# An attention and one-expert kernel: the gates of all tokens computed as if no row were routed, parked in DRAM, two rows replaced there, and reloaded

## The chip, the cores and the metric

The kernel runs on one core of one Trainium2 chip. The metric is the device time of one execution in microseconds (us); the median of three runs of the kernel before is 795.93 us (792.62 to 797.04). Profile times count from the start of the profiled span.

## What is computed

Token rows `x` (2048 rows of 640 values) are normalized to `xn`. Two branches work on `xn`, and the output joins them:

```python
xn = _layernorm(x)
s  = attention(xn)                    # 32 heads of 192, the last 512 keys of a cache, then @ wo
# the routed branch
r   = xn @ w_r                        # one score a token
idx = argsort(-r)[:2]                 # the two best tokens
y   = (silu(x_sel @ w_gate) * (x_sel @ w_up)) @ w_down * sigmoid(r_sel)
z   = xn with y added to the rows idx # 2046 rows stay xn
out = x + s * silu(z)
```

So the gate `silu(z)` is a function of `xn` alone in all rows but two. The kernel uses `silu(z) = z/2 * (1 + tanh(z/2))`.

## The kernel before, in words

**Steps and blocks.** The attention is done in 64 steps: 8 groups of 4 heads, 4 stretches of 512 tokens, 2 pairs of heads. Each step has two halves, called blocks here, numbered 0 to 127. Block b computes scores, exps and products for 256 tokens (two row tiles, a = 0 and 1) and two heads. Blocks 0 to 11 and the last two have an order of their own, written out by hand; blocks 12 to 125 run in the order of the list `BLOCK` (L927). Nothing is reordered: each engine executes its instructions as the program issues them.

```python
BLOCK = "A S0 M0 W m E0 B S1 M1 P E1 l".split()
```

- `A`, `B`: the two phases of the query products for the next step (`q_phase`, L340); after `B`, ScalarE copies them out (L352). Their PSUM pool has one buffer, so the next `A` waits for that copy. Even blocks make two thirds of the query tiles (copy of 1024 columns), odd blocks one third.
- `S0`, `S1`: scores (L367) into one of two PSUM buffers. `M0`, `M1`: row maxima on VectorE (L372). `E0`, `E1`: exps on ScalarE (L377), into one of two buffers `pexp`; behind `E1` SyncE issues the DMA transpose `pT` (L383). The exps of block b+2 write the buffer that the `pT` of block b reads, so they wait for its landing.
- `P`: products with the values for block b-2 (L406), their scaling on VectorE (L413, L417) and ScalarE (L420), and the DMA transpose `oT` (L423).
- `W`: 24 products with `wo` for block b-6 (L447), and their addition to `s_acc` on VectorE (L470). The start of these 24 is used below as the start of a block, W(b).
- `m`, `l` and the middle of `P` are hooks for other work. The lists `mid[b]` run at `m`, after `W` and before `E0` and `M1`; `bg[b]` inside `P` (L948), between its two halves; `end[b]` and then `loads[b]` at `l`.

In `loads` SyncE issues the next group's keys, values and weights (192 to 288 KB each) and `kT` transposes. All these DMAs and both transposes stand in one SyncE queue, in program order.

**The routed branch** (lines 649 to 900) is laid into the hooks. `m_r` makes one column of `r` (L672). `m_round` (L681, mid[28]) rounds it to bf16; `m_rows` (bg[28]) turns it to 16 rows of 128 on TensorE through the query pool (L690) and copies it out on VectorE (L692). `m_top` (end[29]) takes the best of each row (L698 to L703) and spreads them by two GpSimd DMAs; `m_sel`, `m_tok`, `m_own` (end[31], mid[32], end[33]) find the two tokens, and an indirect GpSimd DMA gathers their rows of `x` (L741). `m_gather` (mid and end of 34 to 40) makes a mask `oh` of the two tokens (L758) and normalizes the two rows; its last piece, at mid[40], ends with L774 on VectorE, and loads[40] turns the rows (L778). `m_ffn` does three blocks of 512 hidden columns (bg[42], bg[49], bg[57]): products (L787), a copy and a tanh (L790, L791), one block later two VectorE operations (L797, L798) and a transpose `hT` on SyncE (L801). The weights come through ScalarE's queue. `m_down` (bg[62], bg[69]) and `m_sum` (bg[70]) make the two rows of `y`, put them into DRAM and load them back on all 128 partitions as `y_bc` (L846).

**The gates.** For each of the 16 row tiles n, `m_add(n)` at bg[71+2n] runs five GpSimd operations on `xn` (L850; L853 and L854 twice): halve it, and add each `y` times the mask. `m_gate(n)` then takes the tanh on ScalarE at bg[75+2n] (L860) and, at mid[76+2n], one VectorE operation that leaves the gate in `xn` (L863).

**The end.** From block 107 on, one tile a block: SyncE loads `x_fin` in loads[107+n] (L912), GpSimd makes `s_acc = s_acc * gate + x` at bg[109+n] (L917, L918). The last group's `W`, from block 118, multiplies its products by the gate (L473) and stores.

Of the kernel before, what the change touches and what calls it, by code (L numbers as in the profile page):

```python
# [8 lines left out]
ACT = mybir.ActivationFunctionType  # L9
# [12 lines left out]
def kernel(ctx, tc, A_x, A_k_cache, A_v_cache, A_wq, A_wo, B_x, B_w_r, B_w_gate, B_w_up, B_w_down, out):  # L22
# [149 lines left out]
    eps_t = const.tile([P, 1], FP32, name="eps_t")  # L172
    nc.vector.memset(eps_t, EPS)
    nc.vector.tensor_copy(out=ident, in_=ident_f)
    nc.gpsimd.memset(v_ring[:, :, :, Dh:Dh + 1], 1.0)

    mv = const.tile([P, NTB, 2], FP32, name="mv")
    rstd = const.tile([P, NTB], FP32, name="rstd")
# [470 lines left out]
    def m_open():  # L649
        late.close()  # L650
        M["stack"] = ExitStack()
        M["w"] = M["stack"].enter_context(tc.tile_pool(name="moe_w", bufs=1))
        M["s"] = M["stack"].enter_context(tc.tile_pool(name="moe_s", bufs=1))
        M["wr"] = M["s"].tile([P, D], BF16, name="wr_bc", tag="t3")
        nc.gpsimd.dma_start(out=M["wr"], in_=B_w_r.partition_broadcast(P))
        M["r"] = M["s"].tile([P, NTB], FP32, name="r_pn")
        M["xsT"] = M["s"].tile([P, DC, 32], BF16, name="xsT")
        M["xsel"] = M["s"].tile([32, D], BF16, name="xsel")
        nc.gpsimd.memset(M["xsel"], 0.0)
        M["pick"] = M["s"].tile([P, 2], FP32, name="pick")  # L660
        nc.gpsimd.memset(M["pick"], 0.0)
        for c in range(4):
            nc.gpsimd.affine_select(out=M["pick"], in_=M["pick"], compare_op=ALU.not_equal, fill=1.0, base=-32 * c,
                                    pattern=[[-1, 2]], channel_multiplier=1)
        M["oh"] = M["s"].tile([P, NTB, 2], FP32, name="oh")
        M["iota"] = M["s"].tile([P, NTB], FP32, name="iota")
        nc.gpsimd.iota(M["iota"], pattern=[[P, NTB]], base=0, channel_multiplier=1, allow_small_or_imprecise_dtypes=True)

    def m_r(n):
        def f():  # L670
# [6 lines left out]

    def m_round():

        M["r_b"] = M["s"].tile([P, NTB], BF16, name="r_b")  # L680
        nc.vector.tensor_copy(out=M["r_b"], in_=M["r"])  # L681
        M["base"] = M["s"].tile([NTB, 1], FP32, name="base")
        nc.gpsimd.iota(M["base"], pattern=[[0, 1]], base=0, channel_multiplier=P, allow_small_or_imprecise_dtypes=True)
        M["cpos"] = M["s"].tile([P, NCD], FP32, name="cpos")
        nc.gpsimd.iota(M["cpos"], pattern=[[1, NCD]], base=0, channel_multiplier=0, allow_small_or_imprecise_dtypes=True)

    def m_rows():

        r_ps = f_tile([NTB, P], BF16, "r_ps")
        nc.tensor.transpose(out=r_ps, in_=M["r_b"], identity=ident)  # L690
        M["rows"] = M["s"].tile([NTB, P], FP32, name="r_rows", tag="t2")
        nc.vector.tensor_copy(out=M["rows"], in_=r_ps)  # L692

    def m_top():

        top = M["s"].tile([NTB, 8], FP32, name="top8")
        loc = M["s"].tile([NTB, 8], U32, name="loc8")
        nc.vector.max(out=top, in_=M["rows"])  # L698
        nc.vector.max_index(out=loc, in_max=top, in_values=M["rows"])
        cand = M["s"].tile([NTB, 2, 2], FP32, name="cand")  # L700
        nc.vector.tensor_copy(out=cand[:, 0, :], in_=top[:, 0:2])
        nc.vector.tensor_copy(out=cand[:, 1, :], in_=loc[:, 0:2])
        nc.vector.tensor_scalar(out=cand[:, 1, :], in0=cand[:, 1, :], scalar1=M["base"][:, 0:1], scalar2=None, op0=ALU.add)  # L703
        c_d = tc.dram_tile([NTB, 2, 2], FP32, name="c_d")
        nc.gpsimd.dma_start(out=c_d, in_=cand)
        M["cand"] = M["w"].tile([P, NTB, 2, 2], FP32, name="cand_bc", tag="w")
        nc.gpsimd.dma_start(out=M["cand"].rearrange("p n k c -> p (n k c)"), in_=c_d.rearrange("n k c -> (n k c)").partition_broadcast(P))
# [24 lines left out]
    def m_own():  # L732
        sel = M["s"].tile([2, 2, 2], FP32, name="sel")
        for q in range(2):
            nc.vector.tensor_tensor(out=sel[:, q, :], in0=M["best"][0:2, q, :], in1=ident_f[0:2, 0:2], op=ALU.mult)
        M["own"] = M["s"].tile([2, 2], FP32, name="own")
        nc.vector.reduce_sum(out=M["own"], in_=sel, axis=AX.X)
        idx_i = M["s"].tile([2, 1], I32, name="idx_i")
        nc.vector.tensor_copy(out=idx_i, in_=M["own"][:, 1:2])
        M["xg"] = M["s"].tile([2, D], BF16, name="xg", tag="t2")  # L740
        nc.gpsimd.indirect_dma_start(out=M["xg"], out_offset=None, in_=x_f,  # L741
                                     in_offset=bass.IndirectOffsetOnAxis(ap=idx_i[:, 0:1], axis=0),
                                     bounds_check=S - 1)
# [9 lines left out]

    def m_gather():

        def mask():
            for j in range(2):
                nc.vector.tensor_scalar(out=M["oh"][:, :, j], in0=M["iota"], scalar1=M["best"][:, 1, j:j + 1], scalar2=0.5,  # L758
                                        op0=ALU.is_equal, op1=ALU.mult)

        def begin():
            M["mv2"] = M["s"].tile([2, 2], FP32, name="mv2")
            M["rs2"] = M["s"].tile([2, 2], FP32, name="rs2")
            ln_stats(M["xg"], M["mv2"], parts=2)
            M["nw"] = rsqrt_newton(M["mv2"][:, 1:2], M["rs2"][:, 0:1], 2, 1)

        def newton(q):
            for f in M["nw"][3 * q:3 * q + 3]:
                f()

        def apply():
            mv2, rs2 = M["mv2"], M["rs2"]
            ln_nmr(mv2[:, 0:1], rs2[:, 0:1], rs2[:, 1:2])
            nc.vector.tensor_scalar(out=M["xsel"][0:2, :], in0=M["xg"], scalar1=rs2[:, 0:1], scalar2=rs2[:, 1:2], op0=ALU.mult, op1=ALU.add)  # L774
        return [mask, begin] + [lambda q=q: newton(q) for q in range(4)] + [apply]

    def m_xsT():
        nc.sync.dma_start_transpose(out=M["xsT"], in_=M["xsel"])  # L778
# [2 lines left out]
    def m_ffn(fb):  # L781
# [12 lines left out]
        def act():  # L794
            th = M["th"]
            M["h"] = M["s"].tile([P, P], BF16, name="h")
            nc.vector.scalar_tensor_tensor(out=th[:, 2], in0=th[:, 2], scalar=1.0, in1=th[:, 0], op0=ALU.add, op1=ALU.mult)  # L797
            nc.vector.scalar_tensor_tensor(out=M["h"], in0=th[:, 2], scalar=0.5, in1=th[:, 1], op0=ALU.mult, op1=ALU.mult)  # L798

        def turn():  # L800
            nc.sync.dma_start_transpose(out=M["hT"][:, fb * 4:(fb + 1) * 4, :].rearrange("p c t -> p (c t)"), in_=M["h"])  # L801
# [10 lines left out]
    def m_sig():  # L812

        sg = M["s"].tile([P, 2], FP32, name="sg")
        nc.scalar.activation(out=sg, in_=M["best"][:, 0, :], func=ACT.Tanh, scale=0.5)
        nc.vector.tensor_scalar(out=sg, in0=sg, scalar1=0.5, scalar2=0.5, op0=ALU.mult, op1=ALU.add)
        nc.vector.tensor_tensor(out=M["pick"], in0=M["pick"], in1=sg, op=ALU.mult)
        M["wrow"] = M["s"].tile([P, 1], FP32, name="wrow")
        nc.vector.tensor_reduce(out=M["wrow"], in_=M["pick"], axis=AX.X, op=ALU.add)
# [15 lines left out]
    def m_sum():  # L835
# [4 lines left out]
        y_sb = M["s"].tile([2, D], BF16, name="y_sb", tag="t3")  # L840
        nc.gpsimd.tensor_tensor(out=y4[:, 0:2, :], in0=y4[:, 0:2, :], in1=y4[:, 2:4, :], op=ALU.add)
        nc.gpsimd.tensor_tensor(out=y_sb, in0=y4[:, 0, :], in1=y4[:, 1, :], op=ALU.add)
        y_d = tc.dram_tile([2, D], BF16, name="y_d")
        nc.gpsimd.dma_start(out=y_d, in_=y_sb)
        M["y_bc"] = M["w"].tile([P, 2, D], BF16, name="y_bc", tag="w")
        nc.gpsimd.dma_start(out=M["y_bc"], in_=y_d.partition_broadcast(P))  # L846

    def m_add(n):
        def f():
            nc.gpsimd.tensor_scalar(out=xn[:, n, :], in0=xn[:, n, :], scalar1=0.5, scalar2=None, op0=ALU.mult)  # L850
            for j in range(2):
                yh = M["s"].tile([P, D], BF16, name="yh", tag="t1")
                nc.gpsimd.tensor_scalar(out=yh, in0=M["y_bc"][:, j, :], scalar1=M["oh"][:, n, j:j + 1], scalar2=None, op0=ALU.mult)  # L853
                nc.gpsimd.tensor_tensor(out=xn[:, n, :], in0=xn[:, n, :], in1=yh, op=ALU.add)  # L854
        return f

    def m_gate(n):
        def a():
            M["tz"] = M["s"].tile([P, D], FP32, name="tz", tag="t2")
            nc.scalar.activation(out=M["tz"], in_=xn[:, n, :], func=ACT.Tanh)  # L860

        def b():
            nc.vector.scalar_tensor_tensor(out=xn[:, n, :], in0=M["tz"], scalar=1.0, in1=xn[:, n, :], op0=ALU.add, op1=ALU.mult)  # L863
        return a, b

    bg[11].append(m_open)

# [3 lines left out]
        spot(b).append(m_r(n))  # L871
    end[24].append(m_r(15))
    mid[28].append(m_round)
    bg[28].append(m_rows)
    for b, it in enumerate((m_top, None, m_sel, m_tok, m_own, *m_gather())):
        if it is not None:
            spot(29 + b).append(it)
    loads[40].append(m_xsT)
# [15 lines left out]
    bg[69].append(m_down(1))  # L894
    bg[70].append(m_sum)
    for n in range(NTB):
        bg[71 + 2 * n].append(m_add(n))
        a, b = m_gate(n)
        bg[75 + 2 * n].append(a)
        mid[76 + 2 * n].append(b)  # L900


    def fin_open():
# [5 lines left out]
    def fin_load(n):  # L909
        def f():  # L910
            fin_x[n] = fin_pool["x"].tile([P, D], BF16, name="x_fin")
            nc.sync.dma_start(out=fin_x[n], in_=x_v[:, n, :])  # L912
        return f

    def fin_pre(n):
# [101 lines left out]
```

## Time and profile before

| | |
|---|---|
| median of 3 runs | 795.93 us (792.62 to 797.04) |
| the profiled execution | 794.4 us, of which its span is 792.6 us |
| VectorE, ScalarE, GpSimd busy | 75%, 66%, 40% of the span |
| granted TensorE clock | 1.0 |
| DMA transposes `pT`, `oT` | 134 and 126 issues, 4.8 and 3.6 us from issue to landing (median) |
| `x_fin` loads | 16 of 160 KB, 3.5 us to landing (median) |

The page gives each engine's busy time, then the chain of work that ended last, the costliest groups of instructions (busy time, mean duration, and the idle time before them with what ended it) and the DMA issues. A DMA issue is a row of the engine that issued it (SPq is SyncE's queue); its duration is the time for which that queue can do nothing else, and the landing comes later. The timeline rows read: start, duration, engine, line, operation, out<-in, count, and in brackets the idle time before and what ended it.

### The profile page before, as it was taken

The numbers are of one execution on the slowest core, as the hardware profiler recorded it, in microseconds if no ns is written. First come the engines' busy times: TensorE is split into PE (matmuls) and PEld (weight loads), VectorE is DVE, ScalarE is ACT, GpSimd is POOL, SyncE is SP. The second block draws the span as 40 slices with busy tenths as digits, with TensorE's granted clock in tenths as the row PEclk, the third lists the DMA queues.
The fourth block names the chain that finished last, engine by engine and source line by source line (L and its number), as shares of the span: only waits on it lengthen the run. The fifth ranks groups of instructions, "written<-read, shape, count | busy, mean of one in ns | idle before, by whom it ended". The sixth has DMA issues, their size and how long they took to land.

```text
span 792.6 us, 26635 instructions
## 1 busy us (share of the span) xinstructions
PE 778.2 (98%) x11357; PEld 576.8 (73%) x11357; DVE 594.5 (75%) x1091; ACT 526.1 (66%) x952; POOL 313.8 (40%) x248
## 2 busy tenths in 40 slices
PE   8899999999999999999999999999999999999997
PEld 4457677777777776777777777777777777777775
DVE  7898788877777676767666777777777776766785
ACT  6676666666666766666666667767777776666662
POOL 1334111021110101001001499998996413565865
PEclk9999999999999999999999999999999999999999
DMA  9989999799999999999999999989999899999993
GB/s 233 196 175 168 164 188 165 149 191 164 180 205 173 184 221 195 183 178 216 182 206 167 180 190 183 155 158 184 158 191 164 148 190 179 197 185 168 180 173 87
DMA packets 443319, 141.77 MB, mean 179 GB/s; under 512 B 410436, under 2 KB 442696, under 8 KB 443200
## 3 DMA queue, kind: packets, MB, share of 16 engines
q1 hardware_dynamic: 433568, 130.83, 94.6%
q10 hardware_dynamic: 8672, 6.72, 3.4%
q0 software_dynamic: 960, 2.52, 1.1%
q8 instruction: 89, 1.46, 0.8%
q14 instruction: 30, 0.25, 0.1%
HBM read 39.98 MB, written 2.62 MB: 54 GB/s over the span
## 4 chain that ended last, share of the span: by engine, by line
PE 89%; DMA 4%; DVE 3%; ACT 2%; issue 1%; SPq 0%; ACTq 0%; DVEq 0%
PE w L447 25%; PE q_ps L340 23%; PE o_ps L406 20%; PE s L367 19%; DMA pT<-pexp 4%; ACT pexp L377 1%; PE q_ps L309 1%; DVE nm L372 1%; DMA v_sb<-in_A_v_cache_dram 1%; ACT xnT L283 0%; DMA x_in<-in_A_x_dram 0%; PE tp L282 0%; PE gu_ps L787 0%; DVE fin_t L473 0%; DVE fin_o L475 0%
## 5 line engine op out<-in xcount | busy, mean ns | idle before, releaser
L372 DVE TENSOR_REDUCE nm<-s 128x2 f32<-128x1024 f32 x256 | 313.0, 1223 | 123.1 <-PE s L367 117.2
L377 ACT ACTIVATE pexp<-s,nm 128x512 bf16<-128x512 f32 x512 | 324.3, 689 | 110.5 <-DVE nm L372 67.7
L340 PE MATMUL q_ps<-xnT,wq_g 64*128 64x512 bf16 (+1 forms) x2340 | 232.8, 323 | 1.1 <-ACT qT L352 1.0
L447 PE MATMUL w<-wo_g,oT 64*128 64x320 bf16 x3072 | 231.1, 296 | 0.4 <-ACT o_sb L420 0.2
L367 PE MATMUL s<-kT,qT 64*128 64x512 bf16 x1536 | 211.8, 376 | 1.7 <-ACT pexp L377 1.4
L447 PEld LDWEIGHTS <-oT 64*128 64x128 bf16 x3072 | 171.5, 94 | 57.2 <-issue 1.2
L406 PEld LDWEIGHTS <-pT 64*128 64x128 bf16 x4096 | 177.6, 94 | 31.2 <-issue 2.8
L406 PE MATMUL o_ps<-v_sb,pT 64*128 64x193 bf16 x4096 | 195.6, 243 | 3.0 <-DMA pT<-pexp 1.6
L420 ACT ACTIVATE o_sb<-o_ps,rl 128x192 bf16<-128x192 f32 x250 | 91.7, 418 | 126.8 <-DVE rl L413 120.4
L340 PEld LDWEIGHTS <-wq_g 64*128 64x128 bf16 x2340 | 127.2, 99 | 46.4 <-issue 1.9
L151 POOL COPY wo_g<-wo_g 64x1920 bf16<-64x1920 bf16 x32 | 57.7, 1807 | 213.5 <-DMA wo_g<-in_A_wo_dram 178.1
L367 PEld LDWEIGHTS <-qT 64*128 64x128 bf16 x1536 | 85.6, 94 | 55.9 <-issue 2.4
L470 DVE TENSOR_TENSOR s_acc<-s_acc,w 128x320 f32<-128x320 f32 x192 | 85.0, 484 | 32.8 <-PE w L447 32.7
L352 ACT ACTIVATE qT<-q_ps 128x1024 bf16<-128x1024 f32 x114 | 92.5, 811 | 4.8 <-PE q_ps L340 0.2
L417 DVE TENSOR_TENSOR o_sb<-o_ps,rl 128x384 bf16<-128x384 f32 x131 | 73.0, 558 | 4.5
L121 POOL COPY k_perm<-k_raw 128x768 bf16<-128x768 bf16 x30 | 25.1, 851 | 123.9 <-DMA k_raw<-in_A_k_cache_dram 92.7
L853 POOL TENSOR_SCALAR yh<-y_bc,oh 128x640 bf16<-128x640 bf16 x32 | 61.2, 1912 | 4.9 <-DMA y_bc<-y_d 3.3
L854 POOL TENSOR_TENSOR xn<-xn,yh 128x640 bf16<-128x640 bf16 x32 | 45.7, 1429 | 2.7
L413 DVE RECIPROCAL rl<-o_ps 128x2 f32<-128x2 f32 x256 | 30.6, 160 | 12.9 <-PE o_ps L406 7.6
L918 POOL TENSOR_TENSOR s_acc<-s_acc,x_fin 128x640 f32<-128x640 f32 x16 | 22.4, 1399 | 31.5 <-DMA x_fin<-in_A_x_dram 31.1
L850 POOL TENSOR_SCALAR xn<-xn 128x640 bf16<-128x640 bf16 x16 | 30.0, 1873 | 0.8
L478 POOL TENSOR_TENSOR fin_o<-fin_t,s_acc 128x640 bf16<-128x640 f32 x12 | 18.5, 1542 | 17.4 <-DVE fin_t L473 11.0
(132 smaller groups left out, 261.5 us busy)
## 6 DMA issues: line engine op xcount, KB each, us to landing
wo_g<-in_A_wo_dram SPq DMA_DIRECT2D x32, 240.0 KB, 4.2
k_raw<-in_A_k_cache_dram SPq DMA_DIRECT2D x32, 192.0 KB, 3.3
v_sb<-in_A_v_cache_dram SPq DMA_DIRECT2D x32, 192.0 KB, 4.1
wq_g<-in_A_wq_dram SPq DMA_DIRECT2D x14, 288.0 KB, 3.6
wq_g<-in_A_wq_dram SPq DMA_DIRECT2D x14, 192.0 KB, 3.7
x_fin<-in_A_x_dram SPq DMA_DIRECT2D x16, 160.0 KB, 3.5
pT<-pexp SPq DMA_TRANSPOSE x134, 4.8
oT<-o_sb SPq DMA_TRANSPOSE x126, 3.6
```

The lines of the kernel that those rows point to most:

```text
L151: nc.gpsimd.tensor_copy(out=grp[g][("wo", pr)][half(1), cs, :], in_=grp[g][("wo", pr)][half(0), cs, :])
L340: mm = nc.tensor.matmul(q_ps[k][:, 0:n] if type(q_ps) is list else q_ps[:, k, 0:n], lhsT=wq[half(r), dc, c:2 * Dh:3], rhs=xnT[half(r), tok ...
L352: nc.scalar.activation(out=out, in_=q_ps[:, :, 0:n], func=ACT.Copy, scale=scale)
L367: nc.tensor.matmul(s_of[b, a][:, r, :], lhsT=qT_of[i][half(r), c, u * P:(u + 1) * P], rhs=grp[g][("kT", pr)][half(r), :, c, :], start=(c = ...
L372: rm = nc.vector.tensor_reduce(out=nm_of[b, a], in_=s_of[b, a], axis=AX.X, op=ALU.max, negate=True)
L377: nc.scalar.activation(out=p_ring[:, b % 2, a, :, hh, :].rearrange("p (x j) e -> p x j e", x=2), in_=s_of[b, a][:, hh, :].rearrange("p (j ...
L406: nc.tensor.matmul(o_of[b][r][:, a, 0:Dh + 1], lhsT=pT_ring[half(r), b % RP, a, k, :], rhs=v_ring[half(r), (g * PAIRS + pr) % RV, k, 0:Dh ...
L417: nc.vector.tensor_tensor(out=o_sb, in0=src, in1=rl[:, r].unsqueeze(2).unsqueeze(3).to_broadcast([P, 2, 3, HK]), op=ALU.mult)
L420: nc.scalar.activation(out=o_sb[:, a], in_=src[:, a], func=ACT.Copy, scale=rl[:, r, a:a + 1])
L447: nc.tensor.matmul(w_ps[r][:, 0:HD], lhsT=oT_ring[half(r), bs[pr] % RT, c, :], rhs=grp[g][("wo", pr)][half(r), c, cs], start=(pr == 0 and ...
L470: nc.vector.tensor_tensor(out=acc, in0=acc, in1=src, op=ALU.add)
L853: nc.gpsimd.tensor_scalar(out=yh, in0=M["y_bc"][:, j, :], scalar1=M["oh"][:, n, j:j + 1], scalar2=None, op0=ALU.mult)
```

## The change

The mask and the broadcast of `y` go. The gates of all rows are computed as if no row were routed: tanh on ScalarE at bg[71+2n], two GpSimd operations behind it, and a DMA that stores the tile to the DRAM buffer `gate_d` in loads[72+2n]. The two routed rows get their own gate (bg[103]) and an indirect GpSimd DMA writes them over theirs in `gate_d`. Behind each `x_fin` load SyncE reloads the tile of `xn` from there. `r` is turned by a DMA transpose on SyncE instead of on TensorE, and `m_top`, `m_sel` move one hook on (mid[30], mid[32]); `m_tok` and `m_own` run together (end[33]). The normalization of the two gathered rows ends on ScalarE instead of VectorE. The activation of the hidden columns moves from VectorE to GpSimd. A factor of one half moves from these operations into the ones column of the values (2.0, so that `s` comes out halved) and into the sigmoid's constants. The first reload waits for the indirect DMA; an indirect write waits for all stores.

```diff
-    nc.gpsimd.memset(v_ring[:, :, :, Dh:Dh + 1], 1.0)
+    nc.gpsimd.memset(v_ring[:, :, :, Dh:Dh + 1], 2.0)
...
     def m_rows():
-        r_ps = f_tile([NTB, P], BF16, "r_ps")
-        nc.tensor.transpose(out=r_ps, in_=M["r_b"], identity=ident)
-        M["rows"] = M["s"].tile([NTB, P], FP32, name="r_rows", tag="t2")
-        nc.vector.tensor_copy(out=M["rows"], in_=r_ps)
+        M["rT"] = M["s"].tile([P, P], BF16, name="r_rowsT")
+        nc.sync.dma_start_transpose(out=M["rT"], in_=M["r_b"])
     def m_top():
+        M["rows"] = M["s"].tile([NTB, P], FP32, name="r_rows", tag="t2")
+        nc.vector.tensor_copy(out=M["rows"], in_=M["rT"][0:NTB])
...
         def apply():
             ln_nmr(mv2[:, 0:1], rs2[:, 0:1], rs2[:, 1:2])
-            nc.vector.tensor_scalar(out=M["xsel"][0:2, :], in0=M["xg"], scalar1=rs2[:, 0:1], scalar2=rs2[:, 1:2], op0=ALU.mult, op1=ALU.add)
+            nc.scalar.activation(out=M["xsel"][0:2, :], in_=M["xg"], func=ACT.Identity, bias=rs2[:, 1:2], scale=rs2[:, 0:1])
...
         def act():
-            nc.vector.scalar_tensor_tensor(out=th[:, 2], in0=th[:, 2], scalar=1.0, in1=th[:, 0], op0=ALU.add, op1=ALU.mult)
-            nc.vector.scalar_tensor_tensor(out=M["h"], in0=th[:, 2], scalar=0.5, in1=th[:, 1], op0=ALU.mult, op1=ALU.mult)
+            nc.gpsimd.tensor_tensor(out=th[:, 2], in0=th[:, 2], in1=th[:, 0], op=ALU.mult)
+            nc.gpsimd.tensor_tensor(out=th[:, 2], in0=th[:, 2], in1=th[:, 0], op=ALU.add)
+            nc.gpsimd.tensor_tensor(out=M["h"], in0=th[:, 2], in1=th[:, 1], op=ALU.mult)
...
     def m_sum():
-        nc.gpsimd.dma_start(out=y_d, in_=y_sb)
-        nc.gpsimd.dma_start(out=M["y_bc"], in_=y_d.partition_broadcast(P))
+        nc.gpsimd.tensor_tensor(out=M["xsel"][0:2, :], in0=M["xsel"][0:2, :], in1=y_sb, op=ALU.add)
...
+    def gate_of(tz, x, y):
+        nc.scalar.activation(out=tz, in_=x, func=ACT.Tanh, scale=0.5)
+        nc.gpsimd.tensor_tensor(out=tz, in0=tz, in1=x, op=ALU.mult)
+        nc.gpsimd.tensor_tensor(out=y, in0=tz, in1=x, op=ALU.add)
     def m_gate(n):
+        def f():
+            tz = M["s"].tile([P, D], FP32, name="tz", tag="t2")
+            gate_of(tz, xn[:, n, :], xn[:, n, :])
+    def m_away(n):
+        return lambda: nc.sync.dma_start(out=gate_v[:, n, :], in_=xn[:, n, :])
+    def m_own_gate():
+        gate_of(M["y4"][:, 3, :], M["xsel"][0:2, :], M["y_sb"])
+        nc.gpsimd.indirect_dma_start(out=gate_d, out_offset=bass.IndirectOffsetOnAxis(ap=M["idx"][:, 0:1], axis=0),
+                                     in_=M["y_sb"], in_offset=None, bounds_check=S - 1)
...
-    bg[28].append(m_rows)
-    for b, it in enumerate((m_top, None, m_sel, m_tok, m_own, *m_gather())):
+    loads[28].append(m_rows)
+    for b, it in enumerate((None, m_top, None, m_sel, m_tok_own, None, *m_gather())):
...
-        bg[71 + 2 * n].append(m_add(n))
-        a, b = m_gate(n)
-        bg[75 + 2 * n].append(a)
-        mid[76 + 2 * n].append(b)
+        bg[71 + 2 * n].append(m_gate(n))
+        loads[72 + 2 * n].append(m_away(n))
+    bg[103].append(m_own_gate)
...
     def fin_load(n):
             nc.sync.dma_start(out=fin_x[n], in_=x_v[:, n, :])
+            nc.sync.dma_start(out=xn[:, n, :], in_=gate_v[:, n, :])
```

More of the change, by code (lines that the diff above doesn't have):

```diff
@@ L664, in m_open @@
                                     pattern=[[-1, 2]], channel_multiplier=1)
-        M["oh"] = M["s"].tile([P, NTB, 2], FP32, name="oh")
-        M["iota"] = M["s"].tile([P, NTB], FP32, name="iota")
-        nc.gpsimd.iota(M["iota"], pattern=[[P, NTB]], base=0, channel_multiplier=1, allow_small_or_imprecise_dtypes=True)
+        M["r_b"] = M["s"].tile([P, P], BF16, name="r_b")
+        nc.gpsimd.memset(M["r_b"], 0.0)
     def m_r(n):
@@ L678, in m_round @@
     def m_round():
-        M["r_b"] = M["s"].tile([P, NTB], BF16, name="r_b")
-        nc.vector.tensor_copy(out=M["r_b"], in_=M["r"])
+        nc.vector.tensor_copy(out=M["r_b"][:, 0:NTB], in_=M["r"])
         M["base"] = M["s"].tile([NTB, 1], FP32, name="base")
@@ L737, in m_own @@
         nc.vector.reduce_sum(out=M["own"], in_=sel, axis=AX.X)
-        idx_i = M["s"].tile([2, 1], I32, name="idx_i")
+        M["idx"] = idx_i = M["s"].tile([2, 1], I32, name="idx_i")
         nc.vector.tensor_copy(out=idx_i, in_=M["own"][:, 1:2])
@@ L754, in m_gather @@
     def m_gather():
[L756 to L759, printed above, removed]
         def begin():
@@ L773, in apply @@
             ln_nmr(mv2[:, 0:1], rs2[:, 0:1], rs2[:, 1:2])
-            nc.vector.tensor_scalar(out=M["xsel"][0:2, :], in0=M["xg"], scalar1=rs2[:, 0:1], scalar2=rs2[:, 1:2], op0=ALU.mult, op1=ALU.add)
-        return [mask, begin] + [lambda q=q: newton(q) for q in range(4)] + [apply]
+            nc.scalar.activation(out=M["xsel"][0:2, :], in_=M["xg"], func=ACT.Identity, bias=rs2[:, 1:2], scale=rs2[:, 0:1])
+        return [begin] + [lambda q=q: newton(q) for q in range(4)] + [apply]
     def m_xsT():
@@ L815, in m_sig @@
         nc.scalar.activation(out=sg, in_=M["best"][:, 0, :], func=ACT.Tanh, scale=0.5)
-        nc.vector.tensor_scalar(out=sg, in0=sg, scalar1=0.5, scalar2=0.5, op0=ALU.mult, op1=ALU.add)
+        nc.vector.tensor_scalar(out=sg, in0=sg, scalar1=0.25, scalar2=0.25, op0=ALU.mult, op1=ALU.add)
         nc.vector.tensor_tensor(out=M["pick"], in0=M["pick"], in1=sg, op=ALU.mult)
@@ L842, in m_sum, with m_gate, m_tok_own @@
         nc.gpsimd.tensor_tensor(out=y_sb, in0=y4[:, 0, :], in1=y4[:, 1, :], op=ALU.add)
-        y_d = tc.dram_tile([2, D], BF16, name="y_d")
-        nc.gpsimd.dma_start(out=y_d, in_=y_sb)
-        M["y_bc"] = M["w"].tile([P, 2, D], BF16, name="y_bc", tag="w")
-        nc.gpsimd.dma_start(out=M["y_bc"], in_=y_d.partition_broadcast(P))
-    def m_add(n):
-        def f():
[L850 to L854, printed above, removed]
-        return f
[L857 to L864, printed above, removed]
+        nc.gpsimd.tensor_tensor(out=M["xsel"][0:2, :], in0=M["xsel"][0:2, :], in1=y_sb, op=ALU.add)
+        M["y4"], M["y_sb"] = y4, y_sb
+    gate_d = tc.dram_tile([S, D], BF16, name="gate_d")
+    gate_v = gate_d.rearrange("(n p) d -> p n d", p=P)
+    def gate_of(tz, x, y):
+        nc.scalar.activation(out=tz, in_=x, func=ACT.Tanh, scale=0.5)
+        nc.gpsimd.tensor_tensor(out=tz, in0=tz, in1=x, op=ALU.mult)
+        nc.gpsimd.tensor_tensor(out=y, in0=tz, in1=x, op=ALU.add)
+    def m_gate(n):
+        def f():
+            tz = M["s"].tile([P, D], FP32, name="tz", tag="t2")
+            gate_of(tz, xn[:, n, :], xn[:, n, :])
+        return f
+    def m_away(n):
[4 more added lines that the diff above has]
+                                     in_=M["y_sb"], in_offset=None, bounds_check=S - 1)
+    def m_tok_own():
+        m_tok()
+        m_own()
     bg[11].append(m_open)
```

## The prediction

> **What bounds the kernel.** First the page: TensorE is busy 98% of the span at full clock, and it alone. Busy is not peak, so next the chain that ended last, in order of time. Its rows give the start of every block W(b), and from block 12 on the blocks follow at 5.88 and 5.90 us in turn: TensorE at its pace. What lies above that is what can be won. From W(12) to W(125) these are about 7 us, in a few places; some 4 of them are TensorE's own work of the routed branch.
>
> ```profile
> PE 778.2 (98%) x11357; PEld 576.8 (73%) x11357; DVE 594.5 (75%) x1091; ACT 526.1 (66%) x952; POOL 313.8 (40%) x248
> ```
> ```profile
> 253.25 7.19 DMA pT<-pexp
> ...
> 261.11 0.68 ACT pexp L377
> 261.79 0.50 ACT qT L352
> 262.29 0.04 issue
> 262.33 1.26 PE q_ps L340 x10
> ```
> ```profile
> 599.84 1.66 PE w L447 x24
> 601.50 0.88 DVE s_acc L470 x2
> 602.37 1.55 DVE xn L863
> 603.92 0.68 DVE nm L372
> ...
> 605.24 0.56 DVE o_sb L417
> 605.79 0.12 DVE nm L372
> 605.91 0.04 issue
> 605.96 1.11 PE w L447 x13
> ```
>
> The two pieces of chain show the two ways to lose time. In the first a `pT` lands late (260.44), so the exps E0(41) start at 260.52, 2.77 after W(41) = 257.75; the query copy waits behind them and `A` behind the copy: W(42) comes after 6.31 us, 0.42 lost. So exps may start until **W + 2.35** before TensorE loses. In the second, VectorE's work at `m` lasts so long that M1 starts at 603.85, and the scaling behind it holds the next W: W(99) comes 0.41 late. So M1 may start until **W + 3.78**.
>
> Last the timeline of SyncE's queue around block 110:
>
> ```profile
> 675.57 0.64 SPq L146 DMA_DIRECT2D wo_g<-in_A_wo_dram  x1
> 676.25 1.07 SPq L912 DMA_DIRECT2D x_fin<-in_A_x_dram  x1
> 677.49 1.25 SPq L423 DMA_TRANSPOSE oT<-o_sb  x1
> 678.84 3.00 SPq L383 DMA_TRANSPOSE pT<-pexp  x1
> 681.94 1.44 SPq L125 DMA_TRANSPOSE kT<-k_perm  x1
> 683.48 0.82 SPq L912 DMA_DIRECT2D x_fin<-in_A_x_dram  x1
> 684.41 1.80 SPq L423 DMA_TRANSPOSE oT<-o_sb  x1
> 686.31 1.91 SPq L383 DMA_TRANSPOSE pT<-pexp  x1
> ```
>
> From 666 to 708 the queue rests for under 0.2 us between any two rows: it is full. Their starts against the ends of the exps show `pT` of blocks 108 to 115 issued 0.2, 0.7, 1.1, 3.2, 1.9, 2.5, 2.2 and 1.2 us late, and TensorE loses just 0.06. With 4.4 us to landing, the `pT` of 111 lands at 690.74, which is W(113) + 2.35: nothing is left there; 112, 113 and 114 have 0.1, 0.6 and 0.6 left.
>
> **The change, part by part.** A minus is a gain.
>
> *r turned (blocks 28, 29).* L690 goes from TensorE, and with it the wait of the next `A` for the query pool: the chain has r_ps 0.15, the second half of P 0.10 and `A` 0.15 longer than in other blocks, so **-0.40**. The DMA takes its place behind the `wq` of loads[28]. That ends at 191.9; the earlier end of P moves it to about 191.7. The nearest rows are xsT (4.2 us to landing, 1.2 of issue) and hT (4.4 to 5.3), so `r` lands at 195.9 to 197.0; I take 196.2. Now `m_top` waits for it at mid[30], and M1(30) is queued behind it. Its operations took 192.20 to 193.38, plus the cast (0.27): 1.4 us, so M1 starts at 197.6; W(30) is 192.56 (0.40 earlier), allowed is 196.34: **+1.3**. With 5.3 us to landing it is 1.9; with oT's 3.6 (a larger transpose, the quickest row) r is there when VectorE comes to it at 195.27, and the 1.4 us alone cost 0.3. The Trainium skill, VectorE: DVE Perf Modes, section The three transpose paths, gives 390 ns for a 128x128 turn on TensorE and 1309 ns for the DMA's. It prices the operation, not the landing; an estimate by it has r there at about 193.0 and this term at its lower end. The rows here say 3.6 and more.
>
> `m_sel` at mid[32] (203.98 to 204.88, 0.9 us) fits in the 1.2 us that VectorE has free there; `m_tok` and `m_own` together (0.56 + 0.56) fit at end[33] as `m_top`'s 1.18 did at end[29]. The mask (0.6) hid at mid[34]: nothing.
>
> *Two rows normalized on ScalarE (block 40).* At `m` this stands in front of E0(40) and waits for L197 on VectorE, which ends at 254.62 behind the additions of W. E0(40) ran at 253.39. Now: 254.7, plus 0.65 (the tanh of as many columns, 0.75, of which about 0.1 overlaps), so E0 at 255.35; two exps (1.17 to the next start), the copy of 1024 columns (1.02), and `A`(41) starts at 257.6 instead of 256.55: +1.05. The late W(41) pardons the `pT` of the first chain piece, 0.42: net **+0.6** (0.2 to 1.1).
>
> *Activation on GpSimd.* L797 and L798 (0.29 each, three times) leave VectorE, within its free 1.2 us: nothing. On GpSimd three operations of 128x128, about a fifth of L918's 1.40 each, end some 1.3 us after the tanh; SyncE asks for them at `l`, about 7 us later: nothing.
>
> *Gates.* GpSimd does 2 x 1.4 to 1.5 us a tile (L918 1.40, L478 1.54) in place of 2 x (1.91 + 1.43) + 1.87 = 8.6: off the path. The tanhs (0.75) keep their place in `bg` of odd blocks. The first comes 4 blocks sooner and needs the buffer of `yp`, which the DMAs of L839 have read by 438.5, before 443. L863 leaves VectorE, 16 times. It took 0.82 mostly, but 1.53, 1.34 and 1.64 at 507.7, 519.7 and 602.3, and just behind these three W comes 0.30, 0.11 and 0.41 late: **-0.8**.
>
> *Stores (16 of 160 KB, SyncE, even blocks 72 to 102).* An issue costs like x_fin's: 0.40 to 1.31, mean 0.78. The queue rests in most of these blocks; where not (72, 78, 82), the next `pT` has room. The tightest is that of block 73 (landing 465.47, allowed 466.17): **0** (to +0.8). The indirect DMA (1.04 issue, 4.4 landing) is done by about 642; the first reload asks at 665.
>
> *Reloads (16 of 160 KB, blocks 107 to 122).* Each stands in front of the next block's `oT` and `pT`. I price it like the x_fin of blocks 107 to 113: (0.40 + 0.48 + 1.07 + 0.82 + 0.55 + 0.57 + 0.56) / 7 = 0.64. The queue does not rest, so they add up: seven in front of the `pT` of 114 are 4.5, less 0.3 of rest at 107, less its 0.6 of room: 3.6. At 112 it is 5 x 0.64 - 0.3 - 0.1 = 2.8. The largest counts: **+3.6**. Below it is bounded by 0: a `pT` issue lasts 1.3 to 1.9 us in quiet blocks and 2.9 to 3.2 here, so it waits for something that a reload might fill. Above, by the dearest x_fin (1.07): 7 x 1.07 - 0.9 = 6.6. I stay near the mean. From 115 on the queue has about 0.9 us free a block, enough for a reload but not for catching up. The consumers wait off the path: L917 stands two blocks later on GpSimd, the multiplication by the gate 11 blocks later.
>
> The Trainium skill, DMA: Bandwidth & Descriptors, section Issuing engines are not separate DMA queues, says that all DMAs share 16 engines and that a sequencer's issue time is usually small beside the DMA. The rows disagree for this queue (3.00 of issue where 4.4 us land). By the rule this term would be only the data's time; that is rival 1.
>
> **Sum:** -0.4 + 1.3 + 0.6 - 0.8 + 0 + 3.6 = **+4.3 us**. From the profiled execution's 794.4 this is 798.7; from the median, 1.5 higher, 800.2. The profiled one lies among the runs, so I forecast the middle, **799.4**.
>
> **Rivals.**
> 1. *The reloads hide.* Their issue only fills what `pT`'s issue waits for. For: that issue's two lengths. Against: x_fin, same size, same queue, did not keep the lag of 3.2 away. Sum -0.4 + 1.3 + 0.6 - 0.8 = +0.7: about 796.
> 2. *The reloads and stores cost more,* since 160 KB also delay landings: in blocks 41 to 63 the weights on ScalarE's queue (0.16 MB a block, no SyncE issue) went with some 2 us of late `pT`. At the dear price: 4.3 + 3.0 + 0.8 = +8.1: about 803.
> 3. *Not slower:* the DMA engines have room, so a queue with more to issue does it in the same time and small transfers land sooner. It shows at the reloads and at r's turn, and decides if a reload adds under 0.13 us to SyncE's time (0.9 / 7) and r lands within 3.6 us: -0.4 + 0.3 + 0.6 - 0.8 = -0.3, about 794.9. For: oT's landing. Against: xsT and hT, and `pT`s that land in 4.3 us at best.
> 4. *The change does less than it says:* late W at 83, 85 and 99 not from L863 but from `pT`: 0.8 more, about 800.2, within the forecast's own range.
>
> **How the numbers follow.** Forecast with rival 4 (797.2 to 801.5): 0.52, of which 0.30 lies above 799.9 (0.5% over the median, about what a measurement of this kernel can tell from no change) and 0.22 below. Rival 2: 0.22, slower. Rival 1: 0.16, within 0.5%. Rival 3: 0.05, within. A gain above 0.5% (under 791.9) needs more than all late `pT`s to vanish: 0.05. So slower 0.52, same 0.43, faster 0.05. The sum's ends are -0.4 + 0.3 + 0.2 - 0.8 = -0.7 and -0.4 + 1.9 + 1.1 - 0.8 + 0.8 + 6.6 = +10.2, or 794.5 and 805.4 from the middle of the two bases; the range leaves a little out at each end: 795.0 to 804.5.
>
> **What would show it.** Right: W(29) 5.9 after W(28); W(31) about 1.3 late, with M1(30) behind a wait for r's transpose; E0(40) some 3.5 after W(40), behind L197; W(83), W(85), W(99) no longer late; W(112) to W(117) together 3 to 4 us late, with exps waiting for `pT`. Wrong: if SyncE's `pT` issues shrink as reloads come in, or the stores make `pT` late already from 72 on.

## The result, and the profile after

The changed kernel takes 800.14 us (median of 20 runs, 796.5 to 801.8), the kernel before 795.97 us (20 runs): ratio **1.005**, 95% interval 1.004 to 1.006, 4.2 us slower. The span of its profiled execution is 797.3 us, 4.7 more than before's.

The first line of the page answers to the one shown before:

```profile
PE 779.2 (98%) x11356; PEld 577.8 (72%) x11356; DVE 578.2 (73%) x1066; ACT 525.7 (66%) x954; POOL 229.4 (29%) x211
```

VectorE lost 16 us and GpSimd 84 us of work, and nothing came of it: TensorE's work is the same, and what counts is how often it has to wait. So the two traces are set side by side by the starts W(b), and every spacing above 5.88 or 5.90 us is "late time" of that block.

The chain of the changed kernel around block 41, where before's had a late `pT`:

```profile
254.14 0.06 ACT xsel L766
...
254.97 1.23 ACT pexp L377 x2
256.20 0.91 ACT qT L352
257.11 0.04 issue
257.16 0.73 PE q_ps L340 x10
```

Now the normalization stands ahead of E0(40), and the query copy behind the exps holds `A`(41): W(41) comes 1.16 us late.

The chain around block 99, where before's had L863 on VectorE between two W:

```profile
601.27 0.65 PE s L367 x6
601.92 1.63 PE w L447 x24
603.55 1.08 PE q_ps L340 x10
```

W is followed by TensorE's own work; W(99), W(83) and W(85) are on time. SyncE's queue around block 110 (start, duration, engine, line):

```profile
677.80 0.57 SPq L133 DMA_DIRECT2D wq_g<-in_A_wq_dram  x1
678.43 0.64 SPq L146 DMA_DIRECT2D wo_g<-in_A_wo_dram  x1
679.11 1.75 SPq L912 DMA_DIRECT2D x_fin<-in_A_x_dram  x1
680.90 0.43 SPq L913 DMA_DIRECT2D xn<-gate_d  x1
681.50 1.25 SPq L423 DMA_TRANSPOSE oT<-o_sb  x1
682.85 2.65 SPq L383 DMA_TRANSPOSE pT<-pexp  x1
```

The reload itself takes 0.43 us of the queue, and the `pT` of block 110 is issued 2.7 us after its exps (1.1 before). From W(106) to W(117) the late time is 2.47 us, against 0.08 before. The queue's row looks like the forecast; the experiments say that it is not the cause.

### The profile page after: what moved, and what is told of

Same layout as the page of the kernel before. It is cut to its first block, busy times and chain, and to the rows that moved or that the text cites. A ratio compares the mean times of both kernels' runs of the same rounds, so it can differ in the third digit from the quotient of the medians.

```text
span 797.3 us, 26668 instructions
## 1 busy us (share of the span) xinstructions
PE 779.2 (98%) x11356; PEld 577.8 (72%) x11356; DVE 578.2 (73%) x1066; ACT 525.7 (66%) x954; POOL 229.4 (29%) x211
## 4 chain that ended last, share of the span: by engine, by line
PE 79%; DMA 11%; ACT 5%; DVE 4%; issue 1%; ACTq 0%; SPq 0%; DVEq 0%
PE w L447 22%; PE q_ps L340 20%; PE o_ps L406 17%; PE s L367 16%; DMA pT<-pexp 9%; ACT pexp L377 3%; DVE nm L372 1%; PE q_ps L309 1%; DMA v_sb<-in_A_v_cache_dram 1%; ACT qT L352 1%; DMA oT<-o_sb 1%; ACT o_sb L420 0%; ACT xnT L283 0%; DMA x_in<-in_A_x_dram 0%; PE tp L282 0%
## 5 line engine op out<-in xcount | busy, mean ns | idle before, releaser
L340 PEld LDWEIGHTS <-wq_g 64*128 64x128 bf16 x2340 | 126.9, 100 | 51.2 <-issue 6.2
L846 POOL TENSOR_TENSOR tz<-tz,xn 128x640 f32<-128x640 f32 x16 | 22.4, 1402 | 98.3 <-ACT tz L845 98.3
L413 DVE RECIPROCAL rl<-o_ps 128x2 f32<-128x2 f32 x256 | 30.5, 160 | 12.1 <-PE o_ps L406 7.5
L918 POOL TENSOR_TENSOR s_acc<-s_acc,xn 128x640 f32<-128x640 f32 x16 | 22.4, 1402 | 37.2 <-DMA xn<-gate_d 30.0
L919 POOL TENSOR_TENSOR s_acc<-s_acc,x_fin 128x640 f32<-128x640 f32 x16 | 22.4, 1400 | 1.3
L847 POOL TENSOR_TENSOR xn<-tz,xn 128x640 bf16<-128x640 f32 x16 | 22.4, 1399 | 1.3
```

Of the source, the lines that this page charges most:

```text
L340: mm = nc.tensor.matmul(q_ps[k][:, 0:n] if type(q_ps) is list else q_ps[:, k, 0:n], lhsT=wq[half(r), dc, c:2 * Dh:3], rhs=xnT[half(r), tok ...
L413: nc.vector.reciprocal(out=rl[:, r], in_=o_of[b][r][:, :, Dh])
```

## The experiments

Ratios are to the kernel before, with 95% intervals; 0.001 is 0.8 us. Late times come from one profiled execution of each kernel. Two theories of the reloads are set against each other. Theory 1 is the prediction's: a reload costs the time of its issue on SyncE's full queue. Theory 2: it costs the data that the 16 DMA engines have to move.

### No reloads, and neither stores nor reloads

```diff
-            nc.sync.dma_start(out=xn[:, n, :], in_=gate_v[:, n, :])
```

> The changed kernel without its 16 reloads; the stores and the indirect write stay, so the two routed rows keep the gate of an unrouted row. Both theories of the reloads: 2.4 to 3 us less than the changed kernel, ratio to before 1.001 to 1.002. It prices the whole of the reloads, which the kernel with the reloads on GpSimd is set against. A rival that the loss from block 105 on is not the reloads' (stores, or another order of events in this part): less than 1 us off.

Measured: **0.9996** (0.9982 to 1.0011). The reloads are worth 1.005 - 0.9996 = 0.0054, 4.3 us (give or take 1.4): with them goes the whole loss. Both theories had expected less, 2.4 to 3 us.

The second kernel drops `loads[72 + 2 * n].append(m_away(n))` too.

> The changed kernel without the 16 stores and without the 16 reloads (the indirect write stays; the two routed rows keep the gate of an unrouted row). Theory 1 (the stores cost next to nothing, as forecast): within 0.5 us of the kernel without the reloads alone. Rival (the store issues delay pT in blocks 72 to 105; W(105) came 0.74 us later in the changed kernel, with the last store in the block in front of it): 0.7 to 1.5 us less than without the reloads alone, ratio to before 0.9995 to 1.0005.

Measured: 0.9993 (0.9979 to 1.0006), 0.2 us less than without the reloads alone, which the times cannot tell from nothing. Its profile has 0.0 us of late time from W(71) to W(106) where the kernels with stores have 1.2 on average (table below).

### The reloads on another queue

```diff
-            nc.sync.dma_start(out=xn[:, n, :], in_=gate_v[:, n, :])
+            nc.gpsimd.dma_start(out=xn[:, n, :], in_=gate_v[:, n, :])
```

> The changed kernel with one thing moved: the 16 reloads are issued by GpSimd instead of SyncE; the same bytes move at the same blocks. Theory 1 (the reloads cost because each issue takes time on SyncE's full queue in front of pT and oT): the late blocks 112 to 117 go, 2 to 2.5 us off the changed kernel, ratio to before about 1.002, and pT of blocks 108 to 115 lags as before the change (at most about 3 us). Rival (the 160 KB themselves delay the landings of pT and oT on the shared DMA engines): the time stays within 0.5 us of the changed kernel, ratio 1.005, and pT or oT still land late in 111 to 115.

Measured: **1.0063** (1.0045 to 1.008), not faster than the change as it is. Theory 1, mine, fails here. SyncE's queue in this kernel, with no reload in it:

```profile
684.88 0.97 SPq L912 DMA_DIRECT2D x_fin<-in_A_x_dram  x1
685.95 1.39 SPq L423 DMA_TRANSPOSE oT<-o_sb  x1
687.45 3.21 SPq L383 DMA_TRANSPOSE pT<-pexp  x1
690.71 0.63 SPq L146 DMA_DIRECT2D wo_g<-in_A_wo_dram  x1
691.44 0.55 SPq L912 DMA_DIRECT2D x_fin<-in_A_x_dram  x1
692.09 1.25 SPq L423 DMA_TRANSPOSE oT<-o_sb  x1
693.44 3.79 SPq L383 DMA_TRANSPOSE pT<-pexp  x1
```

In these rows the queue still rests for only about 0.1 us between two issues: much of the time that the reloads' issue left free is in `pT`'s issue, 3.21 and 3.79 us where before's trace has 1.91 and 3.2 for the same two. The Trainium skill, DMA: Bandwidth & Descriptors, section Issuing engines are not separate DMA queues, says that DMAs from all engines run on the same 16 and interleave; for these 160 KB transfers the run agrees.

### The same bytes in half the issues

```diff
-            nc.sync.dma_start(out=xn[:, n, :], in_=gate_v[:, n, :])
+            if n % 2 == 0:
+                nc.sync.dma_start(out=xn[:, n:n + 2, :], in_=gate_v[:, n:n + 2, :])
```

> The changed kernel with 8 reloads of two tiles (320 KB) in place of 16 of one: the same bytes, half the issues. Theory 1 (issue time on SyncE): half of the loss by the reloads goes, 1.5 to 2.2 us off, ratio to before 1.0025 to 1.003. Theory 2 (data on the DMA engines): within 0.8 us of the changed kernel, ratio 1.0045 to 1.006.

Measured: 1.0053 (1.0032 to 1.0074), as theory 2 has it: the bytes decide, not the issues.

### The same issues without the bytes, and four times as many

```diff
-            nc.sync.dma_start(out=xn[:, n, :], in_=gate_v[:, n, :])
+            nc.sync.dma_start(out=xn[0:2, n, :], in_=gate_v[0:2, n, :])
```

> The changed kernel with its 16 reloads still issued by SyncE in their places, but each of 2 rows (2.5 KB) instead of 128 (160 KB); so most rows keep the gate that lies in SBUF, and the two routed rows that of an unrouted row. Theory 1 (issue time on SyncE): the 16 issues of about 0.43 us remain, time within 1 us of the changed kernel, ratio to before 1.004 to 1.005. Theory 2 (data: the 16 DMA engines are full from block 104 on, and a reload takes about 0.6 us of them: the reloads on GpSimd's queue had 10.2% of 65 us for 11 of them): as without reloads, ratio below 1.001.

Measured: 1.0016 (1.0004 to 1.0029): 2.7 us better than the change, 1.6 us (give or take 1.5) worse than no reload. Most of the loss went with the bytes, though not all.

```diff
-            nc.sync.dma_start(out=xn[0:2, n, :], in_=gate_v[0:2, n, :])
+            for u in range(4):
+                nc.sync.dma_start(out=xn[2 * u:2 * u + 2, n, :], in_=gate_v[2 * u:2 * u + 2, n, :])
```

> As the kernel with reloads of 2 rows, but four of them a tile: 64 issues on SyncE, 2.5 KB each. It prices SyncE's issue time by itself. Theory 1 (issue time counts): three more issues of 0.4 us in each of blocks 107 to 122; from 107 to 114 at least 7 x 1.2 = 8.4 us more on a queue without rest, 6 us or more over the kernel with one small reload a tile, ratio to before above 1.008. Theory 2 (only what the DMA engines move counts; an issue fills what pT's issue waits for anyway): within 1.5 us of the kernel with one small reload, ratio 1.000 to 1.0035.

Measured: **1.0116** (1.0084 to 1.0148), 8.0 us (give or take 2.7) over the kernel with one small reload. That is theory 1's number: against issues that bring no bytes to speak of, the queue of SyncE is a limit after all. Its rows:

```profile
683.15 1.18 SPq L914 DMA_DIRECT2D xn<-gate_d  x4
684.49 1.25 SPq L423 DMA_TRANSPOSE oT<-o_sb  x1
685.85 1.75 SPq L383 DMA_TRANSPOSE pT<-pexp  x1
687.70 1.89 SPq L125 DMA_TRANSPOSE kT<-k_perm  x1
689.69 1.00 SPq L912 DMA_DIRECT2D x_fin<-in_A_x_dram  x1
690.74 1.72 SPq L914 DMA_DIRECT2D xn<-gate_d  x4
```

`pT`'s issue is down to 1.75 us. The table takes eight blocks with eight reloads: the time from the issue of `pT` 108 to that of `pT` 116, and how long SyncE's issues between these two points lasted, added up from the traces, in us. What is left of the time are gaps between issues.

| kernel | time | all issues | `pT`, 8 issues | reloads | ratio |
|---|---|---|---|---|---|
| before | 47.3 | 43.5 | 21.0 | | |
| no reloads | 47.6 | 43.9 | 22.1 | | 0.9996 |
| one small reload a tile | 48.6 | 45.0 | 18.7 | 2.3 | 1.0016 |
| the change | 51.1 | 47.5 | 22.4 | 4.2 | 1.005 |
| reloads in pairs | 51.2 | 47.7 | 23.7 | 1.7 | 1.0053 |
| reloads on GpSimd's queue | 51.1 | 45.8 | 25.1 | 0 | 1.0063 |
| four small reloads a tile | 55.5 | 50.6 | 18.0 | 9.6 | 1.0116 |

How much one execution says: the seven profiles without reloads (those of the last experiments below among them) have 47.1 to 47.6 us of time and 20.2 to 22.1 of `pT`.

With 160 KB a block, eight blocks take about 51.1 us whether SyncE spends 4.2, 1.7 or 0 us on issuing them. Where the reloads left SyncE's queue, `pT`'s issue took 2.7 us of the 4.2, and gaps 1.7. The reading is that `pT`'s issue holds a wait for the DMA engines. Small issues eat that wait first (22.1 to 18.7 and 18.0) and then add in full: 9.6 + 1.2 of more gaps, less 4.1, is most of the 7.9 that the last row has over no reloads. A 160 KB reload fills its own issue time with data that the engines must move, 3.5 / 8 = 0.44 us each, so nothing is eaten. Open: whether a small transfer costs the engines something too; only its issue is seen here.

What the DMA engines did from 660 to 725 us (queue: packets, MB, the time of the packets as a share of 16 engines' time), first in the kernel before, then in the change, then with the reloads on GpSimd's queue, which is q0:

```profile
q1 hardware_dynamic: 37209, 11.63, 102.1%
```
```profile
q1 hardware_dynamic: 37099, 12.80, 105.9%
```
```profile
q1 hardware_dynamic: 35471, 11.13, 98.7%
q0 software_dynamic: 528, 1.80, 10.2%
```

The engines were as good as taken before any reload came. A sum over 100% means that packets overlap, so the share does not say how much room was left, and the inside of an issue is seen in no trace: the wait for the engines is argued from these sums and from the experiments. What the experiments show by themselves is that with 160 KB a tile the loss follows the bytes, not the queue and not whether they come in one issue or in half of one a tile. Nor does it follow the number of packets: on GpSimd's queue eleven reloads took 528, which is 48 each, and on SyncE's a reload of 128 rows takes one a row (1280 bytes).

### Three blocks later

```diff
-        loads[107 + n].append(fin_load(n))
-        bg[109 + n].append(fin_pre(n))
+        loads[110 + n].append(fin_load(n))
+        bg[111 + n].append(fin_pre(n))
```

> The changed kernel with x_fin and the reload of tile n at block 110 + n instead of 107 + n, and the two operations on s_acc at 111 + n instead of 109 + n; nothing else is changed. Both theories: six transfers of 160 KB leave blocks 107 to 112, where SyncE's queue and the DMA engines are full, and stand at 123 to 125. At 0.6 us of the DMA engines each that is 3.6 us; 2.5 to 4 us off the changed kernel, ratio to before 1.000 to 1.002. Rival (the excess only moves on to blocks 113 to 120, because the queue has no rest there either): less than 1 us off, ratio 1.004 or more.

The load of `x_fin` moves together with the reload behind it. Measured: 1.006 (1.0043 to 1.0077); the expectation of both theories was wrong, the rival's number came. In its profile W(107) to W(117) are late by only 0.34 us in sum, but W(122) by 0.63, W(128) comes 0.87 later than in the change, and from W(133) to the end it takes 8.7 us, 7.4 before. The load was moved to where the last `pT` are issued, and the loss with it.

### The normalization back on VectorE

```diff
-            nc.scalar.activation(out=M["xsel"][0:2, :], in_=M["xg"], func=ACT.Identity, bias=rs2[:, 1:2], scale=rs2[:, 0:1])
+            nc.vector.tensor_scalar(out=M["xsel"][0:2, :], in0=M["xg"], scalar1=rs2[:, 0:1], scalar2=rs2[:, 1:2], op0=ALU.mult, op1=ALU.add)
```

> The changed kernel with the normalization of the two gathered rows back on VectorE, in its place at mid[40]; everything else stays. Theory 1 (ScalarE's operation in front of E0(40), which waits for VectorE, costs): E0(40) starts within 2.4 us of W(40), W(41) no longer comes 1.16 late, W(42) comes 0 to 0.43 late again; 0.7 us less than the changed kernel (0.7 to 1.2), ratio to before 1.004. Rival (the late pT of block 39 sets E0(41) whatever ScalarE does): W(42) takes the loss over in full, less than 0.2 us off.

Measured: 1.0048 (1.003 to 1.0066), too wide to show 0.7 us. The profile does: W(41) is on time, W(42) 0.09 late; W(40) to W(43) has 1.00 of late time, and in all eight kernels with ScalarE's operation 1.94.

### Only what gained

Kernels without stores and reloads: `y` is added by masks as before, GpSimd makes the gate, the two rows are normalized on VectorE, and `r` is still turned by the DMA transpose.

```diff
-            nc.vector.scalar_tensor_tensor(out=xn[:, n, :], in0=M["tz"], scalar=1.0, in1=xn[:, n, :], op0=ALU.add, op1=ALU.mult)
+            nc.gpsimd.tensor_tensor(out=M["tz"], in0=M["tz"], in1=xn[:, n, :], op=ALU.mult)
+            nc.gpsimd.tensor_tensor(out=xn[:, n, :], in0=M["tz"], in1=xn[:, n, :], op=ALU.add)
```

> The kernel before with the parts of the change that gained, and without its transfers: no store, no reload; y is added by the mask on GpSimd as before (four operations a tile, the halving goes into the constants), the tanh stays on ScalarE, the gate is made by two GpSimd operations instead of VectorE's one (L863). r is turned by the DMA transpose, m_top and what follows move one more odd or even place (end[31], end[33], mid[34]), the mask is made at end[41], and the two rows are normalized on VectorE. Theory: W(29) 0.4 sooner, W(31) on time, W(83), W(85) and W(99) on time: 1.2 us less than before, ratio 0.9985. Rival (GpSimd, now busy for some 9.5 of the 11.8 us of a tile, slows VectorE's operations where both read SBUF): late W between blocks 72 and 106, no gain or up to 1 us slower, ratio 1.000 to 1.0015.

Measured: 1.0048 (1.003 to 1.0065), a miss. Two blocks are late by 2.4 us each. W(34) waits for a `pT` that lands after 8.07 us, while the candidates are being spread. At 78 it is the new work; ScalarE and TensorE rows of the timeline (brackets: idle time before, and what ended it):

```profile
483.31 0.74 ACT L862 ACTIVATE tz<-xn 128x640 f32<-128x640 bf16 x1 [3.63 <-POOL xn L866]
...
484.72 1.53 PE L447 MATMUL w<-wo_g,oT 64*128 64x320 bf16 x20 [2.26 <-ACT o_sb L420]
```

The tanh needs a buffer that GpSimd still reads, and behind it on ScalarE stand the scaling and the exps. So the tanh went one tile later:

```diff
-        bg[75 + 2 * n].append(a)
-        mid[76 + 2 * n].append(b)
+        k = 77 + 2 * n if n < 14 else 90 + n
+        bg[k].append(a)
+        mid[k + 1].append(b)
```

> The kernel with masks on GpSimd, with the tanh one tile later (bg[77 + 2n]). Theory 1 (the wait of the tanh for GpSimd at block 78 cost 2.4 us): W(78) on time, 2.4 us off, ratio to before 1.0015 to 1.002, so that what is left over before lies in the part around block 33, where the spread of the candidates (two GpSimd DMAs) now meets the pT of block 32 that landed after 8.07 us. Rival (that landing was chance): W(34) on time too, ratio 0.9985 to 1.000.

Measured: 1.0011 (0.9985 to 1.0036): the time lies between the two forecasts and its interval holds both. In the profile W(78) is on time, and W(34) too with the same code, so the landing of 8.07 us belonged to that execution (the rival).

The last one is the kernel before with this gate alone: `r`, the two rows and the activation stay as they were.

> The kernel before with one part changed: the gate is made by two operations on GpSimd instead of L863 on VectorE, with the halving taken out of GpSimd's work (constants), and the tanh one tile later (bg[77 + 2n]), so that ScalarE does not wait for GpSimd, as it did at block 78 in the kernel with masks on GpSimd (2.4 us). No transfer is added. Theory (L863 cost 0.8 us at W(83), W(85) and W(99)): 0.8 us less than before, ratio 0.999, these three on time. Rival (GpSimd's longer work, 9.5 us a tile, delays what VectorE or SyncE waits for): 0.5 to 2 us slower, ratio 1.0005 to 1.0025.

Measured: 0.9998 (0.9979 to 1.0017). The expected 0.999 lies inside, and so does nothing. W(85) and W(99) are on time; W(83) is still 0.22 late, with M1(82) behind a query copy on ScalarE, though on time to 0.07 in the eleven other kernels without L863. No kernel tried is shown to beat the one before.

### The kernel before, a second profile

> The kernel before once more, unchanged, for a second profile. Theory (the late blocks that the sum counted as gains belong to the program): W(29) 0.40 late and W(99) 0.41 late again, behind r_ps and behind L863; W(83) and W(85) late by 0.1 to 0.3 again. Rival (some of them are late pT, which fall elsewhere in every execution): W(42), 0.42 late behind the pT of block 39 in the first profile, is on time, and W(83) or W(85) too.

One execution, span 795.9 us (792.6 in the first). W(29), W(83) and W(85) are late by the same 0.40, 0.30 and 0.11; W(99) by 0.81 (0.41 in the first), its L863 now 1.97 us long:

```profile
604.02 0.87 DVE s_acc L470 x2
604.90 1.97 DVE xn L863
606.87 0.26 DVE nm L372
```

W(42) is late by 0.06, not 0.42, and W(61) by 1.10, where the first profile had nothing. So VectorE's and TensorE's delays belong to the program, the late `pT` in part to the execution: between W(43) and W(71) the fourteen profiles hold 3.95 to 7.23 us.

## Why the prediction was right in its number

The time lay 0.7 us above the forecast of 799.4, and the sum of +4.3 met +4.2. The steps did less well than the sum. With fourteen profiles, each term can be read as the mean late time of its stretch in kernels with and without that part (us):

| stretch | part | without | with | difference | forecast |
|---|---|---|---|---|---|
| W(28) to W(40) | r turned by DMA, `m_top` at mid[30] | 0.39 (3 kernels) | 0.56 (9) | +0.17 | +0.9 |
| W(40) to W(43) | two rows on ScalarE | 0.97 (6) | 1.94 (8) | +0.97 | +0.6 |
| W(82) to W(100) | L863 | 1.00 (2), with it | 0.17 (4), without it | -0.83 | -0.8 |
| W(71) to W(106) | stores | -0.01, 0.17, -0.01 | 0.20, 0.77, 0.25 (8) | +1.07 | 0 |
| W(106) to W(117) | reloads of 160 KB | 0.29 (7) | 3.15 (4) | +2.86 | +3.6 |

(In the row on stores the three numbers are W(71) to W(82), to W(100), to W(106); the kernel whose tanh waited is left out of the first.) The differences add up to +4.2, as measured, but the agreement is in part luck. Single stretches differ between executions by some tenths and more: the 3.15 of the reloads holds 4.5 from the kernel with GpSimd's queue, of which 2.8 stand at W(116), behind one `pT` that took 7.9 us to land. W(43) to W(71), where the sum has only the activation and puts it at nothing, differs by 1.5 us between the two profiles first compared; with the activation on GpSimd its mean is 5.3 us (11 kernels), without 5.7 (3), so nothing is seen of the activation. And the times split the loss another way: the reloads 4.3 us (give or take 1.4) for 2.9 here, everything else -0.3 (-1.4 to +0.9, no reloads against before) for +1.4 here. What the times confirm on their own is the reloads.

The forecast's range was meant to lie inside the sum's two ends. The upper end is added wrongly: its own terms give +9.2 us, which is 804.4, not +10.2 and 805.4.

1. **Reloads.** The step that failed: "each stands in front of the next block's `oT` and `pT`", priced by issue time. Size near, cause wrong, and that the two prices lie so near is luck: 0.64 us of issue forecast for a reload, 0.44 of data found. The late time of W(112) to W(117), forecast as 3 to 4 us, was 2.5. The runs put the data in its place: equal loss on another queue, equal loss with half the issues, most of it gone with the bytes. Rival 1 had seen half of it, that issue fills what `pT`'s issue waits for; it went wrong where it took this to make the reloads free. The bytes of a reload make that wait longer by about as much as its issue takes. The prediction set the rows of issue time (3.00 us) against the rule of the Trainium skill, DMA: Bandwidth & Descriptors, section Issuing engines are not separate DMA queues; for these transfers the rule was the better guide (1.0063 on another queue, 1.005 on SyncE's), and the long issue was itself a sign that the engines were full. The prediction tied that rule to rival 1 and so to no loss; but the data's time was not nothing where the engines had no room.
2. **Stores.** "Nothing, to +0.8" was too low: late `pT` came above all at W(77), W(93) and W(98) in kernels with stores, about 0.8 us in the means: the exps in front start within 0.1 us of the landing and later than W + 2.35. That is one of the two signs of being wrong that the prediction named. The other 0.25 us is W(105), 0.6 to 0.7 late in three kernels, and no `pT`: in the change the one it needs lands 1.6 us after W(104), in time, but L413 on VectorE starts 0.7 us late; why stays open. I had looked for room in SyncE's queue, which was there; the late landings say that the data had none. The timed pair (0.9993 against 0.9996) neither shows nor excludes 1.1.
3. **r's transpose.** The +1.3 rested on a landing 4.5 us after the issue. In the changed kernel it was issued at 191.71, and VectorE's cast found it landed at 194.85. The timeline rows of SyncE, then of VectorE:

```profile
191.71 1.15 SPq L687 DMA_TRANSPOSE r_rowsT<-r_b  x1
```
```profile
194.85 0.21 DVE L694 CAST r_rows<-r_rowsT 16x128 f32<-16x128 bf16 x1
...
196.21 1.21 DVE L372 TENSOR_REDUCE nm<-s 128x2 f32<-128x1024 f32 x1
```

So 3.1 us, and 2.9 to 3.2 in all ten kernels whose trace has this landing; M1(30) waited for no transpose, and only `m_top`'s own 1.4 us held it: W(31) came 0.28 late, the lower end (0.3) that the prediction gave. The gain at W(29) was the forecast 0.40. The landing was the mis-sized term: taking the nearest rows (xsT, hT) over the quickest (oT) was the mistake.

4. **Two rows on ScalarE.** W(41) +1.16 against +1.05. The pardon of 0.42 at W(42) was counted from one execution; it was chance, and the term is +1.0.
5. **L863.** The three blocks came late in both profiles of the kernel before. W(83) and W(85) are on time in all without L863, but for the one W(83) above. W(99) is on time in eight of the twelve and 0.1 to 0.4 late in four, with L863 gone, so a late `pT` can stand in its place there. Rival 4 holds at most for a part. That the three were worth 0.8 us is read from profiles; no time shows it (0.9998 with L863 gone).
6. **"No catching up".** The queue recovered by block 118; the lag of `pT` fell from 4.5 us at 111 to 0.5 at 118. The late TensorE gave it time for that: blocks 112, 113, 115 and 117 were 0.5 to 0.8 us longer.

## What to carry to other kernels

- Read a DMA issue that lasts longer than its shortest in the same trace as a wait first, not as a cost of issuing. Before pricing a new transfer by its issue time, ask what that wait is for: if the engines are full, price the bytes, and another queue will not help; if issues are many and small, price the issues.
- To tell the two apart, keep the issues and drop the bytes, keep the bytes and halve the issues, then take the time of some blocks and the queue's issues in it: what the time follows is the limit.
- Take a gain that rests on one late landing only after a second profile of the same kernel; here the delays behind an engine's own work came back in both profiles, while of the late landings some came back (W(62)) and some did not (W(42)).

## What the runs showed of the hardware

- The issue of a `pT` takes 1.2 to 5.4 us on SyncE in these traces, and grows when another engine's queue issues transfers (eight of them: 25.1 us, against 20.2 to 22.1 in the seven profiles without reloads).
- A `pT`, 4.6 to 5.0 us to landing in the median of a profile, took 7.9, 8.1 and 8.2 us in three executions; behind them W came 2.8, 2.5 and 1.1 us late.
- An issue of 2.5 KB takes SyncE 0.29 us, one of 160 KB 0.43 and one of 320 KB 0.43 (medians): the bytes hardly show in it.
